# Reordering one segment of a recurrent-attention kernel: scores behind the first value chunk, fillers in one piece, four spreading loads for sixteen

## The chip, the cores and the metric

The kernel runs on one core of a Trainium2 chip, in one launch. The metric is device time in microseconds (us), the median of a few executions. Five engines work side by side, each through its own queue in order: PE (matmuls; its weight loads are shown as PEld), DVE (vector), ACT (activations, copies), POOL (gpsimd) and SP, which here only issues DMAs.

## The reference

Two layers alternate, twice: A (segment-recurrent attention) and B (a gated MLP with a 2048 x 2048 spatial matrix). The change touches A alone. Cut to what matters:

```python
for s in range(n_seg):                       # 64 segments of 32 tokens
    h = concat([mem, x[s*32:(s+1)*32]])      # 8 memory rows and 32 tokens, 512 wide
    q, k, v = (einsum('btd,dhe->bhte', h, W) for W in (Wq, Wk, Wv))   # 32 heads x 128
    p = softmax(where(mask, q @ k.T * scale, -1e9))                   # 40 x 40
    o = einsum('bhte,hed->btd', p @ v, Wo)
    mem = o[:8]                              # the next segment's memory rows
    outs.append(o[8:])
```

The memory rows of a segment come out of the output projection of the segment before, so the 64 segments of a layer form one chain, and there are two such layers: 128 segments.

## The kernel before, in words

**A segment** (`segment`, L839) runs over `hA`, the 32 rows (8 memory rows and the first 24 tokens) turned so that PE can use them as weights. Its PE work, in written order, is: four projections of 16 matmuls each (`qk` 0, 2, 1, 3: queries and keys of head halves r = 0 and 1); `scores(0)`; `v_mm(0)`, the values of half 0; `v_mm(1)`; `scores(1)`; then for each half an *output group*: `sums_memory(r)` (row sums for the memory rows, by a matmul with ones) and `pv(r)`; then `sums_tokens`; then `wo_pass`, the output projection of 128 small matmuls; then the next segment's first projection.

**Around it**: ACT copies each projection to SBUF (`rows`), and DVE turns the four copies into `QQ` and `KA` (L859). ACT takes the exponentials (`exps`, L891), DVE masks them into `E` (`close`, L894). ACT copies the values of half 0 to `VA` (L968), DVE those of half 1 (L973). `memory_out(r)` (L940) is a logarithm and an exponential on ACT and a product on DVE into `uT`, which `wo_pass` reads: its first 64 matmuls read half 0, the last 64 half 1. After `wo_pass`, `build_hA` (L827) merges the new memory rows into `pre` and turns them into the next `hA`, two DVE operations for which the next segment's first projection waits. The tokens' outputs (`tok_out`, `last_out`) follow on DVE.

**The last eight tokens of each segment** attend to everything but pass nothing on, so their queries, keys and values are made for four segments at a time: a *block* is four segments (`tb`, `j4` = 0 to 3; here j0 to j3), and the block ahead is projected in small pieces, the *fillers* (`b_units`, L723): six chunks of 16 matmuls over `hB`, two in each of three segments. Values come first (chunks 4, 5), then four chunks whose ACT copies DVE turns (`turns`, L744). `store_v` writes the values to DRAM and `spread_v` loads them back regrouped into `VX`, 16 loads of 16 KB a block. Another filler, `y_part` (L771), is the output projection for the last tokens of 16 segments, with sums into `yB`; it takes the remaining segment, j0, from block 4 on, and all four of the last block. In blocks 0 to 3 j0 has no filler at all (but for the first segment of the first layer, where the values of block 0 are made).

A call of `fill()` takes one piece of a filler: pieces one and two are 4 matmuls each, the third is 8, the fourth 16. Before, `fill(2)` stands between the two output groups, `fill()` behind `sums_tokens`, and `fill()` behind `wo_pass`. `run(copies)` issues the ACT copies of finished chunks, `run(turns)`, at the end of the segment, the DVE turns.

**Rows for layer B**: when 16 segments' last tokens are done, four row tiles come due (`due`), one a segment: `y_load` loads `y_o` and `y_x`, `y_add` (in `spare1`, between `memory_out(0)` and `memory_out(1)` on DVE) sums them, `y_stats` (in `spare2`, ahead of `build_hA` on DVE) takes statistics, `y_norm` (in `tail`) normalises. In the first layer `spare2` also takes the statistics of the rows of block `tb + 2` in j2, and in both layers `spare1` of j3 normalises them and loads them back in other layouts (`rows.apply`: `xn_d`, `preB`, `pre`). `ln_turn` turns `preB` into the next block's `hB`.

**Order**: in layer A the queues of PE, DVE and ACT follow the written order. POOL and SP are ordered by a scheduler, each still in order at run time. At the very start POOL issues all weight loads and builds the masks (`_consts`, L53), in one queue; a weight load waits for the landing of the load eight before it.

Of the kernel before, what the change touches and what calls it, by code (L numbers as in the profile page):

```python
# [8 lines left out]
F32 = mybir.dt.float32  # L9
ACT = mybir.ActivationFunctionType  # L10
ALU = mybir.AluOpType
# [41 lines left out]
def _consts(ctx, tc, c, b_sp):  # L53
# [13 lines left out]
    maskf = tmp.tile([P, 224], F32, name="maskf")  # L67
    nc.gpsimd.memset(maskf[:], 1.0)
    for q in range(0, P, 32):
        blk = maskf[q:q + 32, 0:160].rearrange("p (i q) -> p i q", i=4)[:, :, 8:32]  # L70
        nc.gpsimd.affine_select(out=blk, in_=blk, compare_op=ALU.is_ge, fill=0.0, base=8,
                                pattern=[[0, 4], [1, 24]], channel_multiplier=-1)
        own = maskf[q:q + 32, 160:224].rearrange("p (i q) -> p i q", i=4)
        nc.gpsimd.affine_select(out=own, in_=own, compare_op=ALU.is_ge, fill=0.0, base=0,
                                pattern=[[-8, 4], [0, 16]], channel_multiplier=1)
        nc.gpsimd.affine_select(out=own, in_=own, compare_op=ALU.is_ge, fill=0.0, base=7,
                                pattern=[[8, 4], [0, 16]], channel_multiplier=-1)
        nc.gpsimd.affine_select(out=own[:, :, 8:16], in_=own[:, :, 8:16], compare_op=ALU.is_ge, fill=0.0, base=0,
                                pattern=[[8, 4], [1, 8]], channel_multiplier=-1)
    maskN = cp.tile([P, 2, 224], BF16, name="maskN")  # L80
# [510 lines left out]
class _Ahead:  # L591
# [4 lines left out]
    def regroup(self, VB, VX):  # L596

        for r in range(2):
            t = self.rows.pool.tile([P, DM], BF16, name="ln_xn", bufs=2)
            self.nc.vector.transpose(out=t[:], in_=VB[:, :, r, :])  # L600
            t = t[:].rearrange("p (i b j k) -> p j b i k", i=4, b=4, j=4)
            for j in range(4):
                self.nc.vector.transpose(out=VX[:, j, r, :], in_=t[:, j])
# [35 lines left out]
def a_block(tc, c, rows, front, MV_in, RS_in, MV_out, RS_out, ahead, wo, S, first):  # L639
# [6 lines left out]
    with ExitStack() as ctx:  # L646
# [61 lines left out]

        def spread_v(bs, j):

            for gs in range(4):
                t0 = 32 * gs + 8 * j
                nc.sync.dma_start(bs["VX"][32 * gs:32 * gs + 32, j].rearrange("p r e -> p (r e)"),
                                  rows.vb_d[t0:t0 + 8, :].rearrange("k (i c) -> i k c", i=4))

# [101 lines left out]
        def prep_segment(s):  # L817
# [4 lines left out]
            KX = KXr[s % NKQ]  # L822
            nc.gpsimd.tensor_copy(KX[:].rearrange("p g r (i k) -> p r i g k", i=4).rearrange("p r i g k -> p (r i) g k"),
                                  bs["KTB"].rearrange("p r (i g) k -> p (r i) g k", i=4)[:, :, :, 8 * j4:8 * j4 + 8])
            seg_state[s] = dict(QQ=QQ, KX=KX, VX=bs["VX"])
# [13 lines left out]
        def segment(s, fill, spare1, spare2, tail):  # L839
# [120 lines left out]
            psK = attO[0].tile([P, 2, 512], F32, name="psK")  # L960
            r3, _, read = qk(3, psK[:, 0, :])
            psS = att.tile([P, 2, 512], F32, name="psS")
            scores(0)
            expd = exps(0)
            qk_T(3, r3)
            close(0)
            other_bank(v_mm(0, psK[:, 1, :]), read)
            nc.scalar.copy(VA[:, 0].rearrange("p i e -> p (i e)"), psK[:, 1, :])  # L968
            psW = accB.tile([P, 512], F32, name="psV")
            v_mm(1, psW)  # L970
# [3 lines left out]
            close(1)  # L974
            if first and s == 1:
                ln_turn(1)

# [8 lines left out]
            if not (first and s == 0):  # L986
                fill(2)
            sums_memory(1)
# [3 lines left out]
            memory_out(1)  # L992
            fill()
            run(copies)
# [4 lines left out]
            for r in range(2):  # L999
                rt = Rt[:, :, 256 * r:256 * r + 256]  # L1000
                nc.scalar.activation(out=rt, in_=rt, func=ACT.Exp, scale=-1.0)  # L1001
            spare2()
            if s + 1 < NSEG:
# [36 lines left out]
        for s in range(NSEG):  # L1040
            tb, j4 = s // 4, s % 4
            if j4 == 0:
                q = tb % 4
                more = y_part(tb // 4 - 1, q) if tb > 3 else iter(())
            if first and s == 0:
                more = values(units)
            if j4 > 0 and tb == NB - 1:
                more = y_part(tb // 4, j4 - 1, last=True)
            elif j4 == 1:
                more = b_units(tb + 1)  # L1050
# [3 lines left out]
            def spare1():  # L1054
                if ys:
                    rows.y_add(ys[0], first, nc.vector, nc.sync)
                elif stores:
                    last = yB[tb // 4 - 1][:, 0:1]
                    nc.vector.tensor_copy(last, last)
                    run(stores)  # L1060
# [23 lines left out]
            def tail():  # L1084
                if j4 in (2, 3) and tb + 1 < NB:
                    for j in (0, 1):
                        spread_v(blk_state[tb + 1], 2 * j4 - 4 + j)
                if j4 == 0 and tb + 1 < NB and not (first and s == 0):
                    ln_turn(tb + 1)
                if tb == NB - 1:  # L1090
# [4 lines left out]
                if ys:  # L1095
                    y_norm(ys.pop(0), nc.sync)
                if tb % 4 == 3 and j4 == (tb + 1 < NB) and tb > 4:
                    due.extend(range(tb - 7, tb - 3))

# [63 lines left out]
```

## Time and profile before

| | |
|---|---|
| Time, median of 3 runs (lowest to highest) | 1739.79 us (1738.49 to 1740.55) |
| The profiled execution's own time | 1733.2 us |
| Its span, first to last instruction | 1731.5 us |
| Granted PE clock, mean | 0.996 |
| PE busy | 1625.6 us, 94% |
| DVE, ACT, POOL busy | 66%, 62%, 10% |
| Segments of the first layer A | 32 to 756 us |
| Segments of the second layer A | 888 to 1606 us |

The rest of the span is the two layers B and the start. The profile's matmul ends are modelled, so start times are read here: 16 projection matmuls take 0.865 us from start to start. "Idle before" names what ended an engine's wait. "issue" stands for time in which an engine waited for nothing that the profile shows.

### The profile page before, as it was taken

To read this page: it belongs to the slowest core of one execution; us is meant where nothing else is said; L and a number is where in the kernel's file an instruction comes from. 1 tells how busy PE (TensorE), PEld (TensorE's weight loads), DVE (VectorE), ACT (ScalarE), POOL (GpSimd) and SP (SyncE) were. 2 spreads that over 40 slices of the span, in tenths; PEclk is the share of its full clock that TensorE was granted. 3 is DMA by queue.
4 is the path that set the end of the run, shared out by engine and by line. 5 is a ranking of instruction groups with operands and counts; after the bars stand their busy time and mean duration, and the time that the engine had idled before them with its cause. 6 is when DMAs were issued, how large, how long until landed. Compare 5 with 4: busy or idle time off the path is not lost.

```text
span 1731.5 us, 96045 instructions
## 1 busy us (share of the span) xinstructions
PE 1625.6 (94%) x43730; PEld 964.7 (56%) x43730; DVE 1147.1 (66%) x2645; ACT 1076.0 (62%) x2274; POOL 168.7 (10%) x388
## 2 busy tenths in 40 slices
PE   2999999989999999999989999999999989999999
PEld 1555555556555555566545555555555555555565
DVE  2677676767667766784466666666776767667722
ACT  1677777767777677661047777777777767776500
POOL 6000000000000001021110000000000000001100
PEclk9999999999999999999999999999999999999999
DMA  9211111122112212277941111111221132124796
GB/s 357 82 32 33 32 33 32 32 65 75 33 31 59 85 35 64 63 196 142 213 143 35 35 35 35 35 35 35 89 72 36 35 92 78 38 47 142 151 202 155
DMA packets 213342, 139.39 MB, mean 81 GB/s; under 512 B 138272, under 2 KB 185744, under 8 KB 212936
## 3 DMA queue, kind: packets, MB, share of 16 engines
q1 hardware_dynamic: 204328, 106.12, 24.3%
q0 software_dynamic: 8592, 27.12, 4.6%
q8 instruction: 343, 5.62, 1.3%
q14 instruction: 63, 0.52, 0.1%
q10 hardware_dynamic: 16, 0.01, 0.0%
HBM read 64.93 MB, written 41.39 MB: 61 GB/s over the span
## 4 chain that ended last, share of the span: by engine, by line
PE 71%; DVE 20%; DMA 3%; issue 3%; ACT 2%; POOL 0%; SPq 0%; DVEq 0%; ACTq 0%; POOLq 0%
PE pw L755 13%; PE psK L683 10%; PE pg L374 8%; PE psQ L683 8%; PE psV L683 6%; PE psb L683 5%; PE pz L273 4%; DVE VA L973 4%; PE psm L683 4%; DVE E L894 3%; PE pwB L767 2%; DVE uT L947 2%; PE py L417 2%; PE psT L917 2%; PE psO L908 2%
## 5 line engine op out<-in xcount | busy, mean ns | idle before, releaser
L683 PEld LDWEIGHTS <-hA 128*32 128x32 bf16 x12288 | 323.0, 96 | 325.5 <-DVE hA L831 47.5
L755 PEld LDWEIGHTS <-uT 128*32 128x32 bf16 x16384 | 244.4, 97 | 62.4 <-issue 24.0
L856 ACT CAST rows<-psQ 128x512 bf16<-128x512 f32 x256 | 150.0, 586 | 106.2 <-PE psQ L683 106.1
L859 DVE STREAM_TRANSPOSE QQ<-rows 128x512 bf16<-128x512 bf16 x256 | 176.6, 690 | 33.3 <-ACT rows L856 32.4
L859 DVE STREAM_TRANSPOSE KA<-rows 128x512 bf16<-128x512 bf16 x256 | 178.9, 699 | 21.7 <-ACT rows L856 16.9
L755 PE MATMUL pw<-Wo_high,uT 128*32 128x128 bf16 x8704 | 153.8, 221 | 27.1 <-issue 18.2
L830 DVE CAST_PREDICATED pre<-maskM,pw 128x128 bf16<-128x128 uint16 x126 | 36.6, 290 | 203.1 <-PE pw L755 201.4
L374 PE MATMUL pg<-z,wspT 128*128 128x344 bf16 x1024 | 154.5, 309 | 1.8 <-DMA wspT<-in_B_w_sp_dram 1.8
L1001 ACT ACTIVATE Rt<-Rt 128x512 f32<-128x512 f32 x256 | 147.2, 622 | 4.0
L683 PE MATMUL psQ<-Wq_sb,hA 128*32 128x512 bf16 x2048 | 138.8, 381 | 10.3 <-DVE hA L831 6.1
L683 PE MATMUL psQ<-Wk_sb,hA 128*32 128x512 bf16 x2048 | 137.6, 379 | 0.2 <-issue 0.2
L683 PE MATMUL psm<-Wq_sb,hA 128*32 128x512 bf16 x2048 | 137.3, 379 | 0.0
L683 PE MATMUL psK<-Wk_sb,hA 128*32 128x512 bf16 x2048 | 137.3, 379 | 0.0
L947 DVE TENSOR_TENSOR uT<-psO,Rt 128x384 bf16<-128x384 f32 x256 | 135.9, 531 | 0.9 <-ACT Rt L1001 0.9
L944 DVE TENSOR_TENSOR uT<-psO,Rm 128x128 bf16<-128x128 f32 x256 | 74.5, 291 | 93.2 <-ACT Rm L943 81.3
L891 ACT ACTIVATE S<-psS 128x224 bf16<-128x224 f32 x256 | 92.1, 360 | 69.6 <-PE psS L886 69.3
L683 PE MATMUL psV<-Wv_sb,hA 128*32 128x512 bf16 x2048 | 134.9, 381 | 0.0
L683 PE MATMUL psK<-Wv_sb,hA 128*32 128x512 bf16 x2048 | 134.6, 380 | 0.0
L998 ACT ACTIVATE Rt<-psT 128x1024 f32<-128x1024 f32 x128 | 130.9, 1023 | 0.0
L374 PEld LDWEIGHTS <-wspT 128*128 128x128 bf16 x1024 | 100.1, 98 | 55.2 <-DMA wspT<-in_B_w_sp_dram 2.1
L755 PE MATMUL pw<-Wo,uT 128*32 128x128 bf16 x7680 | 129.5, 219 | 0.3 <-DVE uT L944 0.3
L973 DVE CAST VA<-psV 128x512 bf16<-128x512 f32 x128 | 88.5, 692 | 50.1 <-PE psV L683 50.1
(169 smaller groups left out, 2560.5 us busy)
## 6 DMA issues: line engine op xcount, KB each, us to landing
o_d<-o_sb SPq DMA_DIRECT2D x126, 64.0 KB
vb_d<-front SPq DMA_DIRECT2D x30, 256.0 KB
VX<-vb_d SPq DMA_DIRECT2D x480, 16.0 KB
ln_x<-xd SPq DMA_DIRECT2D x26, 256.0 KB
y_o<-o_d SPq DMA_DIRECT2D x22, 256.0 KB
xd<-y_o SPq DMA_DIRECT2D x22, 256.0 KB
y_x<-xd SPq DMA_DIRECT2D x22, 256.0 KB
Wq_sb<-in_A_Wq_dram POOLq DMA_DIRECT2D x8, 512.0 KB, 7.4
```

Of the source, the lines that this page charges most:

```text
L273: nc.tensor.matmul(pz[:, c0:c1], lhsT=xnT[:, kt, :], rhs=w_in_sb[:, kt, c0:c1], start=(kt == 0), stop=(kt == KT - 1))
L374: nc.tensor.matmul(pg[t][:, k, 0:344], lhsT=wsp[t][:, st, :], rhs=z(st, 344 * k, 344 * k + 344), start=(st == 0), stop=(st == NT - 1))
L683: return [nc.tensor.matmul(ps[32 * cg:32 * cg + 32, :], lhsT=lhs(kt, cg), rhs=rhs(kt, cg), start=(kt == 0), stop=(kt == KT - 1), tile_posi ...
L755: nc.tensor.matmul(po[32 * cg:32 * cg + 32, 0:128], lhsT=lhs[:, h, :], rhs=wo_rhs(h, cg), start=(h == 0), stop=(h == H - 1), tile_position ...
L856: return r, mms, nc.scalar.copy(r[:], ps)
L859: nc.vector.transpose(out=QQ[:, j % 2, :, 0:32] if j < 2 else KA[:, j % 2], in_=r[:])
L891: return nc.scalar.activation(out=S[:, r], in_=psS[:, r, 0:224], func=ACT.Exp, scale=scale)
L944: nc.vector.tensor_tensor(out=hview(uT_cur[:], r, 0, 8), in0=oview(r, 0, 8), in1=rm.rearrange("p g (n q) -> p g n q", q=8), op=ALU.mult)
L947: nc.vector.tensor_tensor(out=hview(uT_nxt[:], r, 8, 32), in0=oview(r, 8, 32), in1=rview(r, 0, 24), op=ALU.mult)
L973: nc.vector.tensor_copy(VA[:, 1].rearrange("p i e -> p (i e)"), psW[:])
L998: nc.scalar.activation(out=Rt[:], in_=psT[:], func=ACT.Ln)
L1001: nc.scalar.activation(out=rt, in_=rt, func=ACT.Exp, scale=-1.0)
```

## The change

The scores of half 0 move behind the values of half 0. `fill(3)`, the first 16 matmuls of the segment's filler in one piece, stands between the two output groups, and no filler is left between `sums_tokens` and `wo_pass`. The turn of a chunk that is finished there is run during `wo_pass`, ahead of `spare2` and `build_hA`. The fillers move between segments: `b_units` takes j0, j1, j2 (in block 0 of the first layer j1, j2, j3, as before), `y_part` takes j3, and the segments without filler are now j3. `ln_turn` moves from the end of j0 into its middle, between `close(0)` and the value copy on DVE. The rows for layer B come due three segments later, in j0 of blocks 8 and 12 (15 as before). The matmuls stay the same in number and size.

The spreading loads become 4 of 64 KB for a block, at the end of j1; for that the values of a group of eight tokens lie token-major instead of group-major. `KX` on POOL follows in two copies of half the size, `regroup` with a strided read, and the mask of these columns (`own`) is now built with a DVE maximum and a DVE copy, on which the last four POOL selections work.

```diff
+    fourth = tmp.tile([P, 4, 32], F32, name="fourth")
+    nc.gpsimd.memset(fourth[:], 0.0)
+    nc.gpsimd.affine_select(out=fourth[:], in_=fourth[:], compare_op=ALU.not_equal, fill=1.0,
+                            base=0, pattern=[[-1, 4], [-4, 32]], channel_multiplier=1)
+    own = maskf[:, 160:224].rearrange("p (i q) -> p i q", i=4)
+    is_own = tmp.tile([P, 4, 1], F32, name="is_own")
+    nc.vector.tensor_reduce(out=is_own[:], in_=fourth[:], op=ALU.max, axis=mybir.AxisListType.X)
+    nc.vector.tensor_copy(own, is_own[:].to_broadcast([P, 4, 16]))
     for q in range(0, P, 32):
...
-        own = maskf[q:q + 32, 160:224].rearrange("p (i q) -> p i q", i=4)
-        nc.gpsimd.affine_select(out=own, in_=own, compare_op=ALU.is_ge, fill=0.0, base=0,
-                                pattern=[[-8, 4], [0, 16]], channel_multiplier=1)
...
+        last = own[q:q + 32, :, 8:16]
+        nc.gpsimd.affine_select(out=last, in_=last, compare_op=ALU.is_ge, fill=0.0, base=0,
+                                pattern=[[1, 4], [4, 8]], channel_multiplier=-1)
...
-            t = t[:].rearrange("p (i b j k) -> p j b i k", i=4, b=4, j=4)
+            t = t[:].rearrange("p (i b j k) -> p j b k i", i=4, b=4, j=4)
...
-        def spread_v(bs, j):
-
-            for gs in range(4):
-                t0 = 32 * gs + 8 * j
-                nc.sync.dma_start(bs["VX"][32 * gs:32 * gs + 32, j].rearrange("p r e -> p (r e)"),
-                                  rows.vb_d[t0:t0 + 8, :].rearrange("k (i c) -> i k c", i=4))
+        def spread_v(bs):
+
+            for q in range(0, P, 32):
+                nc.sync.dma_start(bs["VX"][q:q + 32].rearrange("p j r e -> p j (r e)"),
+                                  rows.vb_d[q:q + 32, :].rearrange("(j k) (i c) -> (k i) j c", i=4, j=4))
...
-            nc.gpsimd.tensor_copy(KX[:].rearrange("p g r (i k) -> p r i g k", i=4).rearrange("p r i g k -> p (r i) g k"),
-                                  bs["KTB"].rearrange("p r (i g) k -> p (r i) g k", i=4)[:, :, :, 8 * j4:8 * j4 + 8])
+            for r in range(2):
+                nc.gpsimd.tensor_copy(KX[:, :, r].rearrange("p g (k i) -> p i g k", i=4),
+                                      bs["KTB"][:, r].rearrange("p (i g) k -> p i g k", i=4)[:, :, :, 8 * j4:8 * j4 + 8])
...
             r3, _, read = qk(3, psK[:, 0, :])
+            other_bank(v_mm(0, psK[:, 1, :]), read)
             psS = att.tile([P, 2, 512], F32, name="psS")
             scores(0)
             expd = exps(0)
             qk_T(3, r3)
             close(0)
-            other_bank(v_mm(0, psK[:, 1, :]), read)
             nc.scalar.copy(VA[:, 0].rearrange("p i e -> p (i e)"), psK[:, 1, :])
+            if first and s == 1 or j4 == 0 and tb + 1 < NB and not (first and s == 0):
+                ln_turn(tb + 1)
             psW = accB.tile([P, 512], F32, name="psV")
...
-            if first and s == 1:
-                ln_turn(1)
...
             if not (first and s == 0):
-                fill(2)
+                fill(3)
             sums_memory(1)
             pv(1)
             psT = att.tile([P, 2, 512], F32, name="psT")
             sums_tokens(psT)
             memory_out(1)
-            fill()
             run(copies)
...
+            run(turns)
             spare2()
             if s + 1 < NSEG:
                 build_hA(s + 1, pw)
...
-            if j4 == 0:
-                q = tb % 4
-                more = y_part(tb // 4 - 1, q) if tb > 3 else iter(())
             if first and s == 0:
                 more = values(units)
-            if j4 > 0 and tb == NB - 1:
+            elif j4 > 0 and tb == NB - 1:
                 more = y_part(tb // 4, j4 - 1, last=True)
-            elif j4 == 1:
+            elif j4 == (3 if tb < NB - 1 else 0) and tb > 3:
+                more = y_part(tb // 4 - 1, tb % 4)
+            elif j4 == (first and tb == 0):
                 more = b_units(tb + 1)
...
-                if j4 in (2, 3) and tb + 1 < NB:
-                    for j in (0, 1):
-                        spread_v(blk_state[tb + 1], 2 * j4 - 4 + j)
-                if j4 == 0 and tb + 1 < NB and not (first and s == 0):
-                    ln_turn(tb + 1)
+                if j4 == 1 + (first and tb == 0) and tb + 1 < NB:
+                    spread_v(blk_state[tb + 1])
...
-                if tb % 4 == 3 and j4 == (tb + 1 < NB) and tb > 4:
-                    due.extend(range(tb - 7, tb - 3))
+                if j4 == 0 and tb > 7 and (tb % 4 == 0 or tb == NB - 1):
+                    due.extend(range(tb // 4 * 4 - 8, tb // 4 * 4 - 4) if tb < NB - 1 else range(NB - 8, NB - 4))
```

More of the change, by code (lines that the diff above doesn't have):

```diff
@@ L72, in _consts @@
                                 pattern=[[0, 4], [1, 24]], channel_multiplier=-1)
-        own = maskf[q:q + 32, 160:224].rearrange("p (i q) -> p i q", i=4)
-        nc.gpsimd.affine_select(out=own, in_=own, compare_op=ALU.is_ge, fill=0.0, base=0,
-                                pattern=[[-8, 4], [0, 16]], channel_multiplier=1)
[L76 to L79, printed above, removed]
+        last = own[q:q + 32, :, 8:16]
+        nc.gpsimd.affine_select(out=last, in_=last, compare_op=ALU.is_ge, fill=0.0, base=0,
+                                pattern=[[1, 4], [4, 8]], channel_multiplier=-1)
     maskN = cp.tile([P, 2, 224], BF16, name="maskN")
@@ L1057, in spare1 @@
                 elif stores:
-                    last = yB[tb // 4 - 1][:, 0:1]
+                    last = yB[max(yB)][:, 0:1]
                     nc.vector.tensor_copy(last, last)
```

## The prediction

> **What bounds the kernel now.** I read the page's chain of waits first, then the waits, then the timelines of PE, ACT and DVE through single segments.
>
> ```profile
> PE 71%; DVE 20%; DMA 3%; issue 3%; ACT 2%; POOL 0%; SPq 0%; DVEq 0%; ACTq 0%; POOLq 0%
> ```
>
> PE is the bound, and a fifth of the chain passes through DVE: those are places where PE waits. Three of them lie in every segment. One segment in j2, on PE (start, duration):
>
> ```profile
> 324.03 1.04 PE L683 MATMUL psK<-Wk_sb,hA 128*32 128x512 bf16 x16
> 324.89 0.27 PE L882 MATMUL psS<-QQ,KA 128*32 128x40 bf16 x16
> 325.02 1.03 PE L683 MATMUL psK<-Wv_sb,hA 128*32 128x512 bf16 x16
> 325.88 1.04 PE L683 MATMUL psV<-Wv_sb,hA 128*32 128x512 bf16 x16
> 326.75 0.27 PE L882 MATMUL psS<-QQ,KA 128*32 128x40 bf16 x16
> 326.98 0.23 PE L908 MATMUL psO<-E,ones 64*128 64x64 bf16 x4
> 327.34 0.62 PE L683 MATMUL psb<-Wq_sb,hB 128*32 128x512 bf16 x8
> 328.01 0.23 PE L908 MATMUL psO<-E,ones 64*128 64x64 bf16 x4
> 329.09 1.01 PE L755 MATMUL pw<-Wo,uT 128*32 128x128 bf16 x60
> ```
>
> Eight filler matmuls take 0.44 (as before wo_pass, 328.65 to 329.09), here 0.67: the second output group waits 0.23 for E. In j1 the wait shows:
>
> ```profile
> 317.65 0.23 PE L908 MATMUL psO<-E,ones 64*128 64x64 bf16 x4 [0.27 <-DVE E L894]
> ```
>
> Then the next segment, j3: its fourth projection starts at 334.39, its scores not at 335.25 but here, 0.24 late, because two turns of 0.64 held DVE up.
>
> ```profile
> 335.49 0.28 PE L882 MATMUL psS<-QQ,KA 128*32 128x40 bf16 x16
> ```
>
> And in rare segments DVE waits for a load, which the 14 spreading loads held up on SP (0.67 each):
>
> ```profile
> 368.69 9.32 SPq L713 DMA_DIRECT2D VX<-vb_d x14
> 381.74 0.38 SPq L212 DMA_DIRECT2D y_o<-o_d  x1
> ```
> ```profile
> 386.77 0.69 DVE L216 TENSOR_TENSOR y_o<-y_o,y_x 128x512 f32<-128x512 f32 x1 [3.71 <-DMA y_o<-o_d]
> ```
>
> ACT and DVE in the same j2 segment give the lags used below:
>
> ```profile
> 326.11 0.59 ACT L968 CAST VA<-psK 128x512 bf16<-128x512 f32 x1
> 327.17 0.36 ACT L891 ACTIVATE S<-psS 128x224 bf16<-128x224 f32 x1 [0.47 <-PE psS L886]
> 327.46 0.28 ACT L942 ACTIVATE Rm<-psO 128x128 f32<-128x128 f32 x1
> ```
> ```profile
> 326.97 0.69 DVE L973 CAST VA<-psV 128x512 bf16<-128x512 f32 x1 [0.25 <-PE psV L683]
> 327.58 0.38 DVE L894 TENSOR_TENSOR E<-S,maskN 128x448 bf16<-128x448 bf16 x1
> ```
>
> **The change part by part.** The sum is made against the profiled execution, 1733.2 us (span 1731.5 and 1.7 around it); the median, 1739.8, is 0.4% above, and I carry the difference over as it is. Sums over segments are of starts on PE's timeline.
>
> 1. Scores behind the first values. From the fourth projection's start to scores(0) should be 0.865; over 127 segments the excess is 20.0 (most of it in j3 and j0, 0.23 each, 0.7 beside y_norm). With 0.865 of values between, no excess reaches 0.865. Gain 20.0; bounds 17 and 20.
>
> 2. Filler in one piece. The excess of the first eight filler matmuls over 0.44, in 112 segments with a filler, sums to 34.1. Afterwards 16 matmuls (0.865) stand there. E of half 1 is set by psV and the DVE copy after it, and psV starts when it did (325.88): E ends at 327.96, the second group arrives after 328.2. Gain 34.1; bounds 24 and 34. What is late next: wo_pass follows sums_tokens directly, and its second half needs memory_out(1). The segments without filler have that order already: there sums_tokens starts at 136.16, wo_pass at 136.54, its matmul 61 at 137.39, 0.85 later, as elsewhere. So nothing there.
>
> 3. What step 1 delays. scores(0) starts at 325.75 instead of 324.89. By the lags above ACT's exponential starts 0.42 later, the next ACT instruction 0.29 after that, and the value copy of 0.59 ends at 327.05. The first output group writes the bank that this copy reads and could start at 326.98; with 0.05 from the copy's end to PE (as from E, 327.96 to 328.01), it starts at 327.10. Loss 0.12 x 127 = 15. Bounds: nothing, if the copy comes 0.12 sooner; 0.25 x 127 = 32, if exponential and copy don't overlap. close(0) ends near 326.93 and is in time.
>
> 4. Turn ahead of build_hA. Memory rows are merged 2.02 after wo_pass starts, and the end filler (0.92) covers exactly merge, turn and wait, so what DVE does later than that is paid in full. wo_pass would start near 328.99, the merge is due at 331.0. ACT copies the chunk after memory_out(1), until 329.95; DVE turns it to 330.6. Without statistics that is in time. With one row's (0.72 and 0.18, L134 and L135) DVE is free at 331.5: 0.49 late. By the changed order this holds in 24 segments (the first layer's j2 in 14 blocks, and y_stats in j1 or j2), two of them with two rows' statistics (0.9 more). Loss 24 x 0.49 + 2 x 0.9 = 13.6; bounds 6 and 20.
>
> 5. Four loads for sixteen. SP spends 10 us a block on spreading before, some 4 x 0.67 = 2.7 after (bounds 2.7 and 4 times that). The waits of wo_pass for uT behind y_add sum to 9.8 in four segments. Some comes back: y_norm now follows a turn (0.62), so y_load is issued near 2.9 us into the segment, lands 5.0 later (381.74 to 386.75) and y_add wants it at 6.9. That wait of 1 is half hidden ahead of memory_out(1): 3 in some eight segments. Gain 6.8; bounds 2 and 9.8.
>
> 6. The start. POOL's last four selections now wait for the DVE copy of own, which stands on DVE behind the first turn of hB, and that waits for preB:
>
> ```profile
> 24.34 0.31 DVE L607 STREAM_TRANSPOSE hB<-preB 128x128 bf16<-128x128 bf16 x1 [16.67 <-DMA preB<-xn_d]
> ```
>
> Behind these selections POOL has 22 of 31 weight loads; before, they went out from 11.45 on. The nine in front are landed at 17.6 (the ninth, issued at 10.32, took 7.3); only then do the small preB packets flow freely, so own comes near 19.5, the selections end near 20.8, first bytes 1.5 later. The DMA queues run dry for some 5 us, and the first segment's wo_pass ends when Wo_high is landed (52.5 before, with 0.4 to spare). Values in front of scores don't help, as the weights set the end. Loss 5; bounds -1 (values of 0.86 inside POOL's wait, no hole) and 8.
>
> 7. Instruction fetch. "issue" stalls of 0.3 to 1.4 in or after wo_pass sum to some 35. Taking eight filler matmuls from in front of wo_pass leaves the fetch about 0.2 less, in some 15 cases: loss 3; bounds -3 and 8.
>
> 8. POOL's three copies now fall beside E in three segments of four instead of two. E takes 0.36 alone; beside a POOL copy 0.38 or 0.60. 0.22 more ends at 328.2, inside the filler; in j0, where ln_turn (0.29) stands in front, some 0.03. Loss 1; bounds 0 and 5. The Trainium skill ("SBUF — State Buffer", on the shared port pair) says that the loser blocks for the other's full instruction; this trace shows 0.22 and not the 0.40 of the copy. By the rule E would be 0.40 late, 0.1 to 0.2 past the filler in 93 segments, some 11 instead of 1; I go by the row.
>
> 9. At nothing: ln_turn's earlier place (preB's last load issues about 1 us into j0, the turn wants it at 5.5; if a load is 2 later, 0.5 in single segments); regroup's strided reads (16 transposes of 0.27, behind loads that are later still; doubled, 4); yB sums (0.68) in j3, where no turn is left.
>
> Sum: 20.0 + 34.1 + 6.8 - 15 - 13.6 - 5 - 3 - 1 = 23.3 saved: 1710 for the profiled execution, 1716.5 on the median.
>
> **Rivals.** *The transposes hide.* If copy and turn come earlier, or fetch stalls in wo_pass give DVE time, steps 4 and 6 cost little: 1716.5 - 13 = 1703, to 1698. For: DVE is 66% busy. Against: the end filler leaves 0.05.
> *The fetch takes the gain.* The stalls follow PE's pace; what is removed in front of a fetch returns in it, with step 8 at its bound: 1716.5 + 8 + 4 = 1728, to 1736. For: 35 us of stalls. Against: most removed waits lie far in front of wo_pass.
> *Slower: the first output group behind the ACT copy.* One mechanism, L908 for half 0 waiting on exponential and copy. Each 0.1 costs 12.7; it decides from 0.12 + 23.3/127 = 0.30 a segment on. Without overlap on ACT 0.25 gives 1733; with E late by another 0.15 beside POOL's first half copy, 0.40, 1752. Against: ACT has nothing else to do there.
> *It doesn't do what it says*: the waits of steps 1 and 2 keep their size because another operand ends them. Then only losses and gains of the rest stay, near 1740. Against: the lines name KA and E.
>
> **How the numbers follow.** Forecast 50% (its own range 1709 to 1726), hidden transposes 21%, fetch 16%, slower 10%, no effect 3%. Left out below 1700 are some 8%, above 1736 some 12%: range 1700 to 1736. About 0.2% (3.5 us) is what a measurement can tell from no change: faster 0.86, same 0.04, slower 0.10.
>
> **What would show it.** Step 1: scores(0) 0.13 before psV in every segment, no wait for KA. Step 2: no L908 wait for E of half 1. Step 3: 0.1 before L908 of half 0, ended by ACT VA. Step 4: PE waiting for hA by 0.5 in 24 segments. Step 5: no L216 wait above 1. Step 6: POOL idle until near 20, DMA share falling at 18. Wrong would make me a large new wait at L908 or L928, or loads of preB later than ln_turn.

## The result, and the profile after

The changed kernel takes 1724.3 us in the median against 1739.7 for the kernel before, a ratio of 0.991 (95% interval 0.988 to 0.993). Run once more beside the kernel before, it took 1716.1 against 1735.0: 0.990 (0.988 to 0.992). That is about 17 us faster, inside the predicted range of 1700 to 1736, and less than the 23.3 us of the forecast. Each ratio in this document is to the kernel before on the same chip; 0.001 is 1.7 us.

The chain of waits on the page of the changed kernel, shares of the span by engine, was 71% PE and 20% DVE before:

```profile
PE 82%; DMA 6%; issue 4%; DVE 3%; ACT 3%; SPq 1%; POOL 1%; DVEq 0%; POOLq 0%; ACTq 0%
```

DVE has all but left the chain. PE's timeline through one segment, a j3 with `y_part` as its filler (start, duration), to be read against the j2 segment in the prediction:

```profile
607.34 1.03 PE L687 MATMUL psK<-Wk_sb,hA 128*32 128x512 bf16 x16
608.21 1.04 PE L687 MATMUL psK<-Wv_sb,hA 128*32 128x512 bf16 x16
609.07 0.27 PE L886 MATMUL psS<-QQ,KA 128*32 128x40 bf16 x16
609.20 1.03 PE L687 MATMUL psV<-Wv_sb,hA 128*32 128x512 bf16 x16
610.06 0.27 PE L886 MATMUL psS<-QQ,KA 128*32 128x40 bf16 x16
610.41 0.23 PE L912 MATMUL psO<-E,ones 64*128 64x64 bf16 x4
610.78 1.05 PE L770 MATMUL pwB<-Wo,front 128*32 128x512 bf16 x16
611.76 0.23 PE L912 MATMUL psO<-E,ones 64*128 64x64 bf16 x4
612.39 1.02 PE L758 MATMUL pw<-Wo,uT 128*32 128x128 bf16 x60
```

And ACT, then DVE, in the same segment:

```profile
609.74 0.58 ACT L972 CAST VA<-psK 128x512 bf16<-128x512 f32 x1
```
```profile
609.88 0.39 DVE L898 TENSOR_TENSOR E<-S,maskN 128x448 bf16<-128x448 bf16 x1
610.89 0.38 DVE L898 TENSOR_TENSOR E<-S,maskN 128x448 bf16<-128x448 bf16 x1
```

Three things are to be seen. The scores start 0.86 after the values of half 0, the steady pace, with no wait (609.07). The first output group starts 0.35 after the second scores (610.06 to 610.41), where it was 0.23 before: the ACT copy ends at 610.32. The second group has E from 611.27 on and still starts only at 611.76, 0.98 after the filler began. Sixteen filler matmuls take 0.865, so 0.115 is left that E does not explain.

At the start, the timelines of POOL and of DVE:

```profile
8.24 0.58 POOL L551 DMA_DIRECT2D Wq_sb<-in_A_Wq_dram  x1
19.76 1.40 POOL L82 TENSOR_SCALAR_AFFINE_SELECT maskf<-maskf 32x32 f32<-32x32 f32 x4 [10.94 <-DVE maskf L76]
21.11 1.60 POOL L551 DMA_DIRECT2D Wq_sb<-in_A_Wq_dram  x3
```
```profile
18.84 0.31 DVE L611 STREAM_TRANSPOSE hB<-preB 128x128 bf16<-128x128 bf16 x1 [10.97 <-DMA preB<-xn_d]
19.49 0.20 DVE L76 COPY maskf<-is_own 128x64 f32<-128x64 f32 x1
```

POOL stands for 10.9 us behind the DVE copy, and 22 weight loads stand behind POOL, as the prediction said.

For the rest of the document the segments are cut by the starts of PE's instructions and summed over 125 of them (all but the first of the first layer and the last of each layer; the expectations say 124 or 126 for about the same set). "4th projection" goes from its start to the next stage; "scores, values" to the first output group; "groups" holds both output groups, the filler between them, the token sums and any filler behind them; "behind" holds the last filler and the next two projections. "First segment" is the time at which the first segment ends. One profiled execution each, in us:

| kernel | 4th projection | scores, values | groups | wo_pass | behind | first segment | span |
|---|---|---|---|---|---|---|---|
| before | 126.7 | 263.1 | 268.3 | 265.5 | 335.7 | 53.8 | 1731.5 |
| changed | 107.5 | 279.3 | 247.4 | 265.3 | 345.3 | 58.7 | 1723.4 |
| changed, second execution | 107.5 | 278.6 | 247.5 | 261.2 | 342.6 | 59.9 | 1715.6 |
| e1 scores first | 112.0 | 263.3 | 244.5 | 257.8 | 354.9 | 60.4 | 1710.8 |
| e2 filler split | 107.5 | 278.7 | 253.0 | 261.9 | 340.5 | 58.0 | 1716.8 |
| e3 before, scores behind | 107.5 | 280.7 | 262.5 | 269.5 | 342.0 | 53.9 | 1731.7 |
| e4 mask | 107.8 | 278.5 | 247.7 | 261.2 | 343.8 | 55.4 | 1712.5 |
| e5 scores first, turn at the end | 126.9 | 263.4 | 244.3 | 256.2 | 347.1 | 60.8 | 1717.7 |
| e6 banks exchanged | 107.7 | 267.9 | 247.7 | 255.4 | 350.4 | 59.3 | 1710.6 |
| e7 sixteen loads | 107.5 | 278.3 | 255.3 | 262.7 | 345.5 | 61.0 | 1728.7 |
| e12 scores first, filler split | 111.8 | 263.2 | 261.2 | 256.2 | 345.3 | 60.6 | 1716.3 |

The first three columns repeat to within 1 us between the two executions of the changed kernel; wo_pass and what is behind it do not (4.1 and 2.7), because stalls fall there that move from one to the other, so that these two are best read together. The profile calls them "issue": PE waits for nothing that it shows. The trace ties them to the fetching of instructions: each of the 55 stalls of the changed kernel's first execution (30.5 us of idle PE) ends 1.24 to 1.57 us after a 16 KB packet of the instruction queue (q8 on the page) has come in, though these packets come some 4.1 us apart; the 43 in the kernel before (23.3 us) end 1.24 to 1.60 after one.

### The profile page after: what moved, and what is told of

Same layout as the page of the kernel before. It is cut to its first block, busy times and chain, and to the rows that moved or that the text cites. A ratio compares the mean times of both kernels' runs of the same rounds, so it can differ in the third digit from the quotient of the medians.

```text
span 1723.4 us, 95738 instructions
## 1 busy us (share of the span) xinstructions
PE 1625.9 (94%) x43707; PEld 967.3 (56%) x43730; DVE 1177.1 (68%) x2647; ACT 1071.5 (62%) x2274; POOL 246.5 (14%) x510
## 4 chain that ended last, share of the span: by engine, by line
PE 82%; DMA 6%; issue 4%; DVE 3%; ACT 3%; SPq 1%; POOL 1%; DVEq 0%; POOLq 0%; ACTq 0%
PE psQ L687 13%; PE pw L758 13%; PE psK L687 12%; PE psb L687 9%; PE psm L687 6%; PE psV L687 6%; PE pg L378 6%; PE pwB L770 3%; PE psO L912 3%; PE pz L277 3%; PE psO L929 2%; PE psT L921 2%; PE psS L886 2%; PE py L421 1%; PE psO L932 1%
## 5 line engine op out<-in xcount | busy, mean ns | idle before, releaser
L758 PEld LDWEIGHTS <-uT 128*32 128x32 bf16 x16384 | 232.8, 97 | 66.1 <-issue 58.7
L827 POOL COPY KX<-old 128x128 bf16<-128x128 bf16 x128 | 68.9, 540 | 493.4 <-PE psS L890 420.5
L946 ACT ACTIVATE Rm<-psO 128x128 f32<-128x128 f32 x256 | 71.1, 278 | 100.3 <-PE psO L932 93.2
L827 POOL COPY KX<-front 128x128 bf16<-128x128 bf16 x128 | 66.2, 525 | 458.9 <-PE psS L890 411.4
```

Of the source, the lines that this page charges most:

```text
L758: nc.tensor.matmul(po[32 * cg:32 * cg + 32, 0:128], lhsT=lhs[:, h, :], rhs=wo_rhs(h, cg), start=(h == 0), stop=(h == H - 1), tile_position ...
L827: nc.gpsimd.tensor_copy(KX[:, :, r].rearrange("p g (k i) -> p i g k", i=4), bs["KTB"][:, r].rearrange("p (i g) k -> p i g k", i=4)[:, :, : ...
L946: nc.scalar.activation(out=rm, in_=psO[r][:, :, 320:384], func=ACT.Ln)
```

## The experiments

**Is the order of the scores worth its 20 us?** e1 undoes it in the changed kernel:

```diff
-            other_bank(v_mm(0, psK[:, 1, :]), read)
             psS = att.tile([P, 2, 512], F32, name="psS")
             scores(0)
             expd = exps(0)
             qk_T(3, r3)
             close(0)
+            other_bank(v_mm(0, psK[:, 1, :]), read)
```

> The changed kernel with the scores of half 0 put back in front of the values of half 0; all else as changed. In the profile of the changed kernel the wait for KA in front of these scores is gone (19.2 us over 124 segments), but the first output group starts 0.12 later in each (15.0 us over the same segments). Theory (both belong to this step, and the second output group no longer waits for E, so nothing absorbs either): the wait of 19 to 20 comes back, the 15 go away, 4 to 5 us slower than the changed kernel, near 1728. Rival one (the delay of the first output group has another cause and stays): 19 slower, near 1743. Rival two (the wait for KA was hidden by something later): no difference, near 1724.

Measured: 1713.9 against 1737.5, ratio 0.987 (0.984 to 0.989): not slower than the changed kernel but some 6 us faster. The theory and both rivals fall. The wait for KA came back with 4.5 us, not 19, while the 15 to 16 of the first output group went away. (The first three columns fall by 14; some of that comes back in the last two, where the stalls are.) So in the changed kernel something else had already removed most of the wait for KA. The candidate was the other edit that touches DVE at the segment's end, the turn that moved ahead of `build_hA`. e5 puts that back as well:

```diff
-            run(turns)
             spare2()
```

> The changed kernel with two edits undone: the scores of half 0 in front of its values, and the turn of the chunk finished between the output groups back at the end of the segment. With the scores alone put in front, the wait for KA came back with 4.5 us (starts of 124 segments) and not with 19, and the kernel was 7 us faster than the changed one. Theory (the wait for KA came from two turns at the end of a segment, so the earlier turn has removed it already, and the order of the scores was given a gain that was gone): with the turn at the end the wait for KA is 17 to 20 again, the merge of the memory rows comes in time again (5 to 10 less around the last filler), sum 5 to 12 slower than with the scores alone in front: 12 to 19 us faster than before. Rival (the wait is short because the one-piece filler or the four loads have freed DVE): the wait for KA stays near 4.5, and the time falls by the 5 to 10 of the merge: 28 to 33 faster than before.

Measured: 1720.4 against 1732.8, ratio 0.994 (0.992 to 0.996), 10 us faster than before, just short of the 12 to 19 of the theory, and some 12 slower than e1, as it said. The fourth projection is at 126.9 again, the value of the kernel before. The rows of PE's waits for KA, of e1 and then of e5 (total us, times, longest):

```profile
PEld L886 <- DVE KA L863: 31.8, 125, 1.3
PE psS L886 <- DVE KA L863: 2.5, 4, 0.8
```
```profile
PEld L886 <- DVE KA L863: 50.6, 125, 1.3
PE psS L886 <- DVE KA L863: 6.7, 12, 0.8
```

The weight load of the scores waits 18.8 us longer with the turn at the end. That settles it: the wait for KA came from two turns behind each other at the end of a segment. Moving one of them away removes 15 of the 19 us; moving the scores removes the same microseconds a second time, and costs 15 at the first output group.

**Why is the first output group late?** e6 exchanges the two accumulators, so that half 0 does not write the banks which the ACT copy of its values still reads:

```diff
-            psO = [attO[r].tile([P, 2, 512], F32, name="psO") for r in range(2)]
+            psO = [attO[1 - r].tile([P, 2, 512], F32, name="psO") for r in range(2)]
```

> The changed kernel with the two accumulators of the output groups exchanged: half 0 now writes the banks that nothing else uses in the segment, half 1 those that hold the fourth projection and the values of half 0, which the ACT copy reads. Theory (the first output group starts 0.12 late in each segment because it waits for that ACT copy, which ends 0.05 after E of half 0): 0.04 to 0.09 less in 126 segments, 5 to 11 us faster than the changed kernel, so 21 to 27 faster than before. Rival one (E of half 0, or the passage between the kinds of matmul, sets the start): no difference, 16 faster than before. Rival two (half 1 keeps its banks until the end of the token outputs, and the next fourth projection now waits for them): slower.

Measured: 1704.5 against 1732.8, ratio 0.985 (0.983 to 0.988). The step from the second scores to the first group falls from 0.35 to 0.26 in the typical segment, "scores, values" by 10.7 to 11.4. The waits name the change of cause. First the changed kernel, then e6:

```profile
PEld L912 <- issue: 55.7, 128, 0.6
```
```profile
PEld L912 <- DVE E L898: 56.1, 127, 0.7
```

In the changed kernel the wait is put down to "issue", nothing that the profile shows; with the banks exchanged it is E of half 0. The theory holds: of the 0.12 per segment, 0.09 was the copy's hold on the bank, and E itself is the 0.03 that is left. Rival two falls too: the fourth projection stays at 107.7.

**The same order, in the kernel before.** e3 is the kernel before with the diff of e1 the other way round.

> The kernel before with one edit: the scores of half 0 behind the values of half 0. Theory (waits in series: the first output group comes 0.12 later, but the second one was waiting for E by 0.19 a segment, so it starts when it did): gain 19 for KA, loss 15 at the first group, of which 12 to 13 come back as a shorter wait for E: 16 to 18 us faster than before, near 1723. Rival (the parts add up, nothing absorbs): 4 to 5 faster, near 1735. Rival two (the order brings nothing): 1740.

Measured: 1734.4 against 1737.5, ratio 0.999 (0.997 to 1.0005), no difference. The first two steps of the theory are in the trace: KA's 19.2 went, 17.6 appeared at "scores, values", and the filler between the groups took 16.7 less (137.5 to 120.8), as a shorter wait for E. But the two output groups themselves grew from 83.4 to 95.5, and wo_pass and what is behind it by 10. PE's weight-load rows show the place of the first of these two (one segment of e3, and the same loads of VX in one of the kernel before):

```profile
328.15 0.14 PEld L908 LDWEIGHTS <-ones 64*128 64x128 bf16 x4
328.21 0.21 PEld L925 LDWEIGHTS <-VA 64*128 64x128 bf16 x8
328.49 0.22 PEld L928 LDWEIGHTS <-VX 64*128 64x128 bf16 x2
```
```profile
327.16 0.10 PEld L928 LDWEIGHTS <-VX 64*128 64x128 bf16 x2
```

The last weight loads, of VX, take 0.22 instead of 0.10. Ahead of them stands an extra semaphore instruction on PE: a chunk of VX, 64 rows for one segment, comes from two of the sixteen loads, and both are waited for, in every segment. The kernel before has the same 241 instructions, and there its first output group hides them (0.36 in the median from its start to the filler; 0.44 in e3). So I expected the four loads to be worth something on PE as well, which the prediction had not seen.

**Four loads or sixteen.** e7 is the changed kernel with sixteen loads in the new layout:

```diff
-            for q in range(0, P, 32):
-                nc.sync.dma_start(bs["VX"][q:q + 32].rearrange("p j r e -> p j (r e)"),
-                                  rows.vb_d[q:q + 32, :].rearrange("(j k) (i c) -> (k i) j c", i=4, j=4))
+            for q in range(0, P, 32):
+                nc.sync.dma_start(bs["VX"][q:q + 32, j].rearrange("p r e -> p (r e)"),
+                                  rows.vb_d[q + 8 * j:q + 8 * j + 8, :].rearrange("k (i c) -> (k i) c", i=4))
```

> The changed kernel with sixteen loads of 16 KB for the spreading again, eight at the end of j1 and eight at the end of j2, into the changed layout. Theory (two costs: SP is held 10 us a block, so that loads of y_o come late, 7 to 9 us of wo_pass waits; and sixteen loads put an extra semaphore instruction on PE ahead of the VX matmuls, 241 of them instead of 61, which shows since the first output group has no slack, 0.07 in some 90 to 120 segments, 6 to 8 us): 12 to 17 us slower than the changed kernel, so level with before to 4 faster. Rival one (only the SP time counts): 7 to 9 slower, 7 to 9 faster than before. Rival two (the loads are hidden): 16 faster than before.

Measured: 1730.5 against 1732.8, ratio 0.9986 (0.997 to 1.000), 15 us slower than the changed kernel at 0.990. The instructions on L932, of the changed kernel and of e7:

```profile
L932 PEldq EVENT_SEMAPHORE  x61: 51/51/51, 97.6 to 1544.4; - x61
```
```profile
L932 PEldq EVENT_SEMAPHORE  x241: 51/51/51, 100.1 to 1583.5; - x121
```

The four loads each serve all four segments of a block, so that only the first segment of a block waits. "groups" grew by 7.8, the median of the first output group from 0.36 to 0.44: the second half of the theory. The first half is not borne out in this execution: PE waits 2.3 us for uT in `wo_pass`, not 7 to 9. So 8 of the 15 us are shown; against the second execution of the changed kernel some 4 more lie in wo_pass and what is behind it, against the first none, and I cannot place them. The Trainium skill ("Perfetto Trace Analysis", Identifying Dependency Chains) says that an instruction with waits on several engines may get such semaphore instructions in front of it. Here the several waits are on loads of one queue; their price, 0.07 a segment, is what these runs add.

**The filler in one piece.** e2 splits it again in the changed kernel, e12 in e1:

```diff
-                fill(3)
+                fill(2)
...
             memory_out(1)
+            fill()
             run(copies)
```

> The changed kernel with eight filler matmuls between the output groups and eight behind the token sums again; all else as changed. Theory (of the 0.30 that I took for the wait for E in each segment 0.11 is a cost of passing from filler matmuls to the output group, which stays; and the output groups now come 0.12 later, so that the wait for E comes back with 0.07 to 0.10 only, 8 to 11 us; the instruction-fetch stalls fall from 30 us to the 23 of before): 1 to 4 us slower than the changed kernel, 1725 to 1728, with stalls named issue near 23. Rival one (the prediction's size, 34 us less 13 for the later group, and fetch 3): 18 slower, near 1742. Rival two (the fetch stalls do not depend on these matmuls): 8 to 11 slower, 1732 to 1735, issue near 30.

> The changed kernel with the scores of half 0 in front of its values and with eight filler matmuls between the output groups and eight behind the token sums. With both output groups at their old times this shows what the filler in one piece removes: in the kernel with the scores behind the values, splitting it cost 5.6 us in the starts around the output groups. Theory (of 34 us some 13 are the passage from filler matmuls to the output group, 0.115 in 112 segments, which stays in any order): the starts around the output groups grow by 18 to 22 us against the kernel with the scores alone in front; the time by 15 to 22, so 1 to 8 us faster than before. Rival one (34 us of wait for E as predicted): 30 or more slower than with the scores alone in front, slower than before by 7 or more. Rival two (5.6 in this order too): 5 slower, 17 to 19 faster than before.

Measured: e2 1721.3 against 1737.5, ratio 0.992 (0.990 to 0.994), about the changed kernel's; e12 1716.4 against 1734.3, ratio 0.990 (0.988 to 0.992), some 5 us slower than e1 (the number of rival two, but not its 5.6 in the starts). In the starts, splitting costs 5.6 us of "groups" in the changed order and 16.7 with the scores in front. That is less than the 8 to 11 of the theory for e2, though its time fits, and nearly the theory for e12 (18 to 22 expected): the late first output group covers most of the wait for E, so the two waits are one stretch of time in two places. The passage from filler to output group can be read by itself: in e2, where E is mostly in time, the first eight filler matmuls take 0.55 from start to start in 86 of 120 segments, 0.11 over their 0.44; in e12 0.65 to 0.69 in 116; in the changed kernel, with sixteen, 0.98 in all 120, again 0.115 over 0.865. In the time, e12 lost only 5 of the 16.7. PE's wait for hA behind the last filler, by the starts, is 2.4 less in e12 than in e1 (6.7 against 9.2). The stalls, as idle time of PE, were 29.9 in e1 and 25.4 in e12; but the changed kernel alone had 30.5 and 22.9 in two executions, so that this pair shows no cause for them. The rest stays open.

**The start.** e4 gives POOL's last selections a tile of their own:

```diff
+    last = tmp.tile([P, 4, 8], F32, name="last")
+    nc.gpsimd.memset(last[:], 1.0)
...
-        last = own[q:q + 32, :, 8:16]
-        nc.gpsimd.affine_select(out=last, in_=last, compare_op=ALU.is_ge, fill=0.0, base=0,
+        l = last[q:q + 32]
+        nc.gpsimd.affine_select(out=l, in_=l, compare_op=ALU.is_ge, fill=0.0, base=0,
...
+    nc.vector.tensor_tensor(out=own[:, :, 8:16], in0=own[:, :, 8:16], in1=last[:], op=ALU.mult)
```

> The changed kernel with POOL's last four selections made on a tile of their own, which DVE multiplies into the mask later, so that POOL waits for no DVE instruction ahead of its weight loads; one DVE product and one POOL memset more. Theory (the wait of 10.9 us on POOL at 19.8 holds 22 weight loads back): no such wait, the first segment starts near 32 instead of 36.3, 4 to 5 us faster than the changed kernel, near 1720. Rival (the loads are bound by bytes and by the landing of earlier ones, so that they end when they do now): no difference, near 1724.

Measured: 1714.7 against 1737.5, ratio 0.987 (0.985 to 0.990), some 5 us faster than the changed kernel. The first segment ends at 55.4 instead of 58.7 or 59.9. POOL's timeline shows no wait between the selections and the loads:

```profile
8.79 0.23 POOL L84 TENSOR_SCALAR_AFFINE_SELECT last<-last 32x32 f32<-32x32 f32 x1
8.98 1.62 POOL L554 DMA_DIRECT2D Wq_sb<-in_A_Wq_dram  x3
```

**The changed kernel again.**

> The changed kernel once more, unedited, since the single edits are judged against its ratio to the kernel before, which stands on 4 runs (0.988 to 0.993). Theory (execution to execution the time of the changed kernel varies by some 4 us with the instruction fetch): ratio 0.989 to 0.993, and stalls named issue between 25 and 31 us in the profile instead of the 30.5 of the first. Rival (the first ratio was off by the chip or by few runs, and the kernels with one edit stand no better than the changed one): 0.985 to 0.988.

Measured: ratio 0.990, as the first time, so the single edits are compared with a firm number. The second profiled execution was 7.8 us shorter than the first (span 1715.6 against 1723.4). PE's waits in `wo_pass`, first and second execution:

```profile
PE pw L758 <- issue: 22.5, 39, 1.6
```
```profile
PE pw L758 <- issue: 17.9, 39, 1.3
```

PE's idle time put down to "issue" was 30.5 in all in the first and 22.9 in the second, which is 7.6 of the 7.8; before it was 23.3. Theory and measurement differ only in that the lower end of the stalls was undercut.

**Faster kernels.** e9 combines e1, e4 and an earlier place for statistics: in the first layer's j2 they stand between the two memory outputs where no row for layer B is added, and the turn goes to the segment's end where there is one.

```diff
-            run(turns)
+            if not ys:
+                run(turns)
             spare2()
...
+                if first and j4 == 2 and tb + 2 < NB and not ys:
+                    _stats(nc, rows.pool, rows.xs[tb + 2], MV_in[:, tb + 2, :])
...
-                    _stats(nc, rows.pool, rows.xs[tb + 2], MV_in[:, tb + 2, :])
+                    if ys:
+                        _stats(nc, rows.pool, rows.xs[tb + 2], MV_in[:, tb + 2, :])
```

> A try at a faster one: the changed kernel with the scores of half 0 in front of its values, POOL's selections on a tile of their own, the first layer's row statistics in j2 moved between the two memory outputs where no row for layer B is added, and the turn at the end of the segment where such a row is. Theory (the parts are separate: 7 us for the scores, 5 for the start, 3 to 7 for the merge of the memory rows): 32 to 36 us faster than before, near 1703. Rival (fetch stalls take the part of the merge back): 27 to 29 faster.

Measured: 1705.1 against 1732.8, ratio 0.984 (0.982 to 0.987), 27 us faster than before: the size of the rival, but not its cause. The fourth projection went from 112.0 in e1 to 116.8, and with it PE's own wait for KA from 2.5 to 6.4 us (4 and 12 times): turns at the end bring it back in this order. "behind" fell from 354.9 to 345.7.

e10 keeps the changed order, which asks for KA late, and combines e6, e4, the earlier statistics of e9 and the turn at the end of the segment in all segments; e11 is e10 with the turn where e9 has it.

> A second try at a faster one: the changed kernel with its order of scores and values, the two accumulators exchanged, POOL's selections on a tile of their own, the first layer's row statistics in j2 between the two memory outputs, and the turn back at the end of the segment. Theory (with the scores behind the values PE asks for KA 0.865 later, so that two turns at the end cost nothing, and the merge of the memory rows is in time): 28 us of the exchange, 5 of the start, 4 to 7 of the merge: 37 to 40 faster than before, no wait for KA over 2 us in all. Rival (the late turns come back at E of half 0 or at KA): 28 to 33 faster.

> The same with the turn ahead of the merge, as in the changed kernel, except in segments that take statistics of a row for layer B there. Theory (the turn ahead of the merge is in time where no statistics stand behind it): within 3 us of the kernel with the turn at the end. Rival (the turn is late in every segment in which a fetch stall or ACT's copy comes late): 4 to 8 slower than that one.

Measured: both 1695.0 against 1734.3, ratio 0.978 (e10 0.975 to 0.980, e11 0.976 to 0.980), 38 us faster than before and 21 faster than the changed kernel. The chain of waits of e10:

```profile
PE 93%; DMA 3%; issue 2%; DVE 2%; ACT 1%; POOL 0%; POOLq 0%
```

The turn's place is worth nothing there, as the theory for e11 says. In e10 the weight loads of the scores wait 6.6 us for KA, where I had allowed 2, but the matmuls themselves never start late for it:

```profile
PEld L889 <- DVE KA L866: 6.6, 19, 0.5
```

With the accumulators exchanged, the scores behind the values are the order of the fastest kernel measured. That this order is the better one is not shown: by the starts e11 is only some 2 us shorter than e9 over all five columns, though 11 us faster in the time, and the scores in front of the values were not run with the accumulators exchanged.

## Why the prediction was right, and where it was not

The range held, and most mechanisms were found where the prediction put them; the largest term was too large and another had a second owner. Against its own sum, in us saved:

| step | predicted | first execution | second |
|---|---|---|---|
| 1 scores behind values (4th projection) | 20.0 | 19.2 | 19.2 |
| 2 filler in one piece, with 8 (groups) | 34.1 - 1 | 20.9 | 20.8 |
| 3 first output group behind the ACT copy (scores, values) | -15 | -16.2 | -15.5 |
| 4 turn ahead of build_hA (behind) | -13.6 | -9.6 | -6.9 |
| 5 and 7 four loads, instruction fetch (wo_pass) | 6.8 - 3 | 0.2 | 4.3 |
| 6 the start (end of the first segment) | -5 | -4.9 | -6.1 |
| layers B and the ends | 0 | -1.5 | 0.1 |
| sum | 23.3 | 8.1 | 15.9 |

The sums are of profiled executions, and that of the kernel before ran 6.5 us below its median (1733.2 against 1739.7), those of the changed kernel within 1.2 of theirs; so the medians show 15.5 and 19.0 saved. That the range held is in part luck: step 2 was 12 to 13 us too large, and step 4 gave some of it back by costing 4 to 7 less than allowed.

**The step that failed is 2.** It took the whole excess over 0.44 as the wait for E. The 34.1 are a mean of 0.28 over 120 segments (the prediction says 112). Of that, 0.11 to 0.115 was the passage from filler matmuls to the output group, which the change leaves where it is: 13 to 14 us, the gap between 34.1 and 20.9. The prediction's j2 segment has 0.67 for eight matmuls, and its group starts 0.05 after E ends; the 0.23 looked like one wait, while the passage ran beside it. Its lower bound of 24 was too high for the same reason. A segment in which E is early, as at 611.76 above, separates the two; of the 120 segments with a filler in the kernel before, one (0.55) has E early, and it would have been enough. Why the passage costs this much no run here shows.

**Step 1** has the right size in the sum and a wrong owner. Its text says that two turns of 0.64 held DVE up, and step 4 moves one of the two: the wait should have been divided there. For the scores' order alone, beside the rest of the change, its steps 1 and 3 give 5 us saved; e1 gained 6 by undoing it, 11 off and of the other sign.

**Step 3** was right in size and cause, and e6 shows the cause: the bank, not the exponential. **Step 6** was right in both; e4 gives back 3.3 to 4.5 us at the end of the first segment.

**Step 4** was too large by 4 to 7, and its row in the table also takes in stalls: counted only where the projection starts right behind hA, the delay sums to 7.1 and 7.7 us in the two executions against 0.9 before. It falls on 13 and 14 segments (over 0.2 each) and not on 24, and is mostly 0.3 to 0.4 and not 0.49; of a segment in the first layer's j2, DVE, then PE and its weight loads:

```profile
557.50 0.71 DVE L747 STREAM_TRANSPOSE front<-rowsB 128x512 bf16<-128x512 bf16 x1 [0.18 <-ACT rowsB L746]
558.14 0.65 DVE L138 BATCH_NORM_STATS2 bnst<-ln_x 128x6 f32<-128x512 bf16 x1
558.92 0.27 DVE L834 CAST_PREDICATED pre<-maskM,pw 128x128 bf16<-128x128 uint16 x1
559.23 0.31 DVE L835 STREAM_TRANSPOSE hA<-pre 128x128 bf16<-128x128 bf16 x1
```
```profile
558.33 1.04 PE L687 MATMUL psb<-Wk_sb,hB 128*32 128x512 bf16 x16
559.59 1.17 PE L687 MATMUL psQ<-Wq_sb,hA 128*32 128x512 bf16 x16 [0.23 <-ACT Rt L1004]
559.59 0.55 PEld L687 LDWEIGHTS <-hA 128*32 128x32 bf16 x15 [0.72 <-DVE hA L835]
```

The filler starts at 558.33 and the projection 1.26 later instead of 0.92: 0.34. The merge comes 0.78 after the statistics start, where the prediction had 0.90. PE's row names ACT's Rt, which ended at about the same time; but in each of these segments the projection starts 0.05 to 0.06 after hA is done, whatever ACT does.

**Step 5**: the waits of `wo_pass` for uT fell from 9.8 to 0.6 and 1.5, a little more than the 6.8, although DVE still waits up to 1.6 and 2.2 for a load of y_o, where the prediction allowed 1. What it left out, the semaphore instructions on PE, was hidden in the kernel before and would show only in the new order (output groups in e3 and e7: 8 to 12 us). **Step 7** forecast a loss of 3, with bounds of -3 and 8: the fetch excess of the starts went from 38.6 to 47.5 in one execution, 8.9 and so just beyond, and to 38.7 in the other. As idle time of PE the stalls were 22.9 to 30.5 over the ten profiled executions with the filler in one piece and 23.3 to 27.4 over the four with a split one, so that no run shows them following the filler's pieces. **Step 8**: POOL's copies now overlap 215 of the 256 products that make E, instead of 64, and the median product takes 0.39 against 0.38 alone; 31 take more than 0.45, as many as before, now 0.46 to 0.52 where it was 0.60. By the Trainium skill's rule of the shared port pair ("SBUF — State Buffer", Terms) a product would be blocked until the copy in front of it is done. Of the 215, 213 begin while a copy runs, with 0.18 of it left in the median, so that they would take some 0.56; the trace does not agree, and the row was the better guide. That a copy holds a product up in part is not excluded: none ends before the copy in which it began.

Of the rivals, the one on the other side needed 0.30 a segment at the first output group; it was 0.12 to 0.13. The one in which the fetch takes the gain needed 8 us of stalls beyond the forecast; they rose by 8.9 in one execution, 6 beyond it, and by 0.1 in the other. The hidden transposes are refuted by steps 4 and 6, which cost 6 to 7 and 5 to 6.

## What to carry to other kernels

Two edits that each shorten the same wait must not both be credited with it: find the engine that holds the wait up, and see which of the edits moves work on that engine. Before an excess over the ideal duration is called a wait, look for a segment in which the awaited operand is early; what remains there is not that wait, and an earlier operand does not take it away. When an instruction moves earlier or later against a copy that reads the same banks, write down who holds each bank; here exchanging two accumulators was worth 9 us for one changed line.

## What was not expected of the hardware

Passing from filler matmuls (128 rows by 32 columns) to the output groups (64 by 128) costs PE 0.115 us beyond their steady pace, with all operands ready. Extra semaphore instructions in PE's weight-load queue, 51 ns each, cost 0.07 in a segment when the scores stand behind the values (e3, e7), and nothing seen in the order before. And one kernel's profiled executions differed by 7.8 us, with instruction-fetch stalls of 30.5 and 22.9 us as PE's idle time, each ending 1.2 to 1.6 us after a packet of instructions had come in: in this kernel a single profile does not show gains below that size, but the starts of single stages do.
